# Turning the keys in four pieces and taking their features in pairs, in an attention and expert kernel of one core

## The chip, the cores and the metric

The kernel runs on one core of a Trainium2 chip. The core has five engines that run side by side and wait for each other by semaphores: TensorE (PE in the profile, its weight loads PEld), VectorE (DVE), ScalarE (ACT), GpSimd (POOL) and SyncE (SP), which here only issues DMAs. The metric is the device time of one execution in microseconds; of several executions the median is given.

## The reference, cut to what matters

```python
def phi(x):                                  # q and k: (4, 4, 1088, 32); S1, S2: (8, 32)
    a = np.einsum('rd,bhsd->bhsr', S1, x)
    b = np.einsum('rd,bhsd->bhsr', S2, x)
    return np.einsum('bhsi,bhsj->bhsij', a, b).reshape(*x.shape[:-1], 64)
q_p, k_p = phi(q), phi(k)
kv = np.einsum('bhsf,bhsd->bhfd', k_p, v)
z = np.sum(k_p, axis=2)
num = np.einsum('bhsf,bhfd->bhsd', q_p, kv)
den = np.einsum('bhsf,bhf->bhs', q_p, z)[..., None] + 1e-06
x = (num / den)                              # -> (4352, 128): 4 batches of 1088 tokens, 4 heads of 32
h = x @ w_in                                 # w_in (128, 2048), w_out (2048, 128)
g = np.where(h > 0, h, np.exp(np.minimum(h, 0)) - 1)
out = (g @ w_out).astype(np.float32)
```

q, k and v come as 32-bit floats, S1, S2, w_in and w_out as 64-bit floats. The kernel turns the 64-bit words into 32-bit floats itself, in several elementwise steps.

## The kernel before, in words

Every batch's 1088 tokens are 17 tiles of 64. A group is 8 such tiles (512 columns of x), and the 4352 tokens make nine groups, the last a smaller one. w_in and w_out are cut into eight blocks of 256 of the 2048 hidden units. A step is one group with one block: `mm1` (x times a block of w_in, into the PSUM tiles `h`), ELU on ACT and DVE (`e`, `gg`), and the second product (`o`, or `pa` and `pb`). The order of all work is written out by hand: the program issues instructions to each engine in the order of the source, an engine runs its own in that order, and `at`, `mid` and `late` hang side work on numbered steps.

**The head** comes before the first step. It loads the keys of batch 0 (`hd_k`, two DMAs: tiles 0 to 8 and 9 to 16), turns them on DVE so that features lie on the partitions (`transp`, L281; a tile of the keys is 64 elements of such a transpose in each partition), and multiplies each turned tile with the sketch matrix `Sab` on TensorE (`KF`, L341). Tile `i` of the lower half of the tokens (u = 0, tiles 0 to 8) goes to the columns 0 to 63 of the array, tile `9 + i` of the upper half (u = 1) to the columns 64 to 127. The results of i = 0 to 4 stand in one PSUM bank, those of i = 5 to 8 in another (`abp`), and ACT copies each bank to `abk` (L349). From there the head goes on: the outer products `kp` of the key features on POOL (L324) and DVE (L411), the sums z (`Z_first` L419, `Z` L257, `Z_out` L450), the first query group's features (`q1_first` L516, `q1z_first` L528), its denominators and products (`q2_den`, `q2_out`: `pw` L603, `den` L608 and L609, `an` L611, `qp` L624), `kv` (`KA`, L428), x of the first group (`xg`, L649) and at last the first `mm1` (L686, L257).

**The weights' 64-bit words** are worked on in between. `RA` (L101) is the first step of a block on DVE, `RB` (L106) the second on ACT, and `RC_2`, `RE` the rest. In the kernel before, `q2_den(0, ...)` issues `RA(0)` between `pw` and `den`; `RA(1)` stands between the two halves of `qp`.

**The weight sums.** From group 2 on (and for the last two blocks of group 1) the second product of a step is done as seven half-size products in place of eight (`mm2_seven`, L792). For that POOL makes sums of the weights once, `SS` (`weights7`, L740, four operations for a range of blocks), and sums of `gg` in every step, `tt` (`sums7`, L751 to L756). The first `mm2_seven` of group 2 takes the products in the order p1, p2, p6, p3, p5, p7, p4; p6 reads `tt` of L755, p4 that of L756. POOL's operations stand in one queue, so what `weights7` takes is ahead of the sums of the next step.

The first steps from step 2 on are (1, 0), (1, 1), then blocks 2 to 5 of groups 0 and 1 in turn; steps 12 to 15 are (0, 6), (0, 7), (1, 6), (1, 7), and group 2 begins with step 16. The second product of a step is issued two steps later.

`keep_warm` issues matmuls on constants whose result nobody reads.

Of the kernel before, what the change touches and what calls it, by code (L numbers as in the profile page):

```python
# [22 lines left out]
def _ap(ap: bass.AP, free):  # L23
    return dataclasses.replace(ap, ap=[list(ap.ap[0])] + [list(x) for x in free])
# [3 lines left out]
def kernel(  # L28
# [28 lines left out]
    NP = NC // 2  # L57
    NT = S // 64
    KT = (NT + 1) // 2
# [12 lines left out]
    kT = [const.tile([FD, 2 * KT, 64], F32, name=f"kT{b}") for b in range(2)] * 2  # L72
# [105 lines left out]
    def round_w(f, i, *a):  # L178
        if wide:
            cp, w_in, w_out = order[i]  # L180
            c = slice(0 if w_in else 2 * P, 4 * P if w_out else 2 * P)
            f(raw_w[cp][:, c], W[:, cp, c], *a)

    def RA(i):
        round_w(round_a, i)
# [75 lines left out]
    def keep_warm(n, cols=256, tile=P):  # L261
        ones = nc.const_aps.tensor(1.0, [P, 256], F32)
        for i in range(n):
            for c in range(0, P, tile):
                nc.tensor.matmul(idle[c:c + tile, :cols], ones[:, :tile], ones[:, :cols], skip_group_check=True,  # L265
                                 tile_position=(0, c))
# [13 lines left out]
    def transp(dst, x, b, t0, t1):  # L280
        nc.vector.transpose(dst[b][:, t0:t1, :].rearrange("p t (a c) -> p c t a", c=2), hd[x, b][:, :, t0:t1, :])  # L281
# [4 lines left out]
    def make_SXh():  # L286
        xps = psum.tile([P, 512], F32, name="SXps", tag="aux")
        nc.tensor.matmul(xps[:, :FD], idr[:].rearrange("p x j -> p (x j)"), Sx[:].rearrange("p h d -> p (h d)"))
        nc.scalar.copy(SXh[:], xps[:, :FD])
        nc.gpsimd.tensor_mul(SXh[:].rearrange("p (h d) -> p h d", h=H), SXh[:].rearrange("p (h d) -> p h d", h=H),  # L290
                             _ap(hmask[:], [[1, H], [0, D]]))
# [9 lines left out]
    sps = psum.tile([P, 512], F32, name="sps", tag="aux")  # L301
    nc.tensor.matmul(sps[:, :2 * R], Sx[:].rearrange("p h d -> p (h d)"), ident[:, :2 * R])
    make_SXh()
    transp(kT, "k", 0, 0, 2)
    nc.vector.tensor_mul(Sab[:], _ap(sps[:, :2 * R], [[0, H], [1, 2 * R]]), _ap(bmask[:], [[1, H], [0, 2 * R]]))
    nc.gpsimd.tensor_copy(SW[:, :, :2, :].rearrange("p h x r -> p h (x r)"), Sab[:])

# [26 lines left out]
    def KF(b):  # L334
        ps = [psum.tile([P, 512], F32, name="abp", tag="h", bufs=4) for _ in range(2)]

        part = [(range(5), 0), (range(3), 1)]
        todo = [(i, u) for r, u in part for i in r] + [x for i in range(5, KT) for x in ((i - 2, 1), (i, 0))]
        todo += [(i, 1) for i in range(KT - 2, KT)]
        for i, u in todo:  # L340
            nc.tensor.matmul(ps[i // 5][64 * u:64 * u + 64, 64 * (i % 5):64 * (i % 5) + 64],  # L341
                             kT[b][:, u * KT + i, :], Sab[:].rearrange("p h y -> p (h y)"),
                             skip_group_check=True, tile_position=(0, 64 * u))
        kf_ps.extend(ps)
        ab = feats[b] = work.tile([P, 2, KT, H, R], F32, name="abk", tag="abk", bufs=2)
        for j in range(2):
            t = slice(0, 5) if j == 0 else slice(5, KT)
            n = t.stop - t.start
            nc.scalar.copy(ab[:, :, t].rearrange("p x t h r -> p x (t h) r"),  # L349
                           ps[j][:, :64 * n].rearrange("p (m x r) -> p x m r", x=2, r=R))  # L350
# [172 lines left out]
    def q1z_first():  # L523
        p = psum.tile([P, 512], F32, name="zqp", tag="h", bufs=4)
        for i in range(4):
            for u in range(2):
                b, t = half_tile(0, 2 * i + u)
                nc.tensor.matmul(p[64 * u:64 * u + 64, i * 32:i * 32 + 32].rearrange("p (h r) -> p h r", h=H),  # L528
                                 qT[b][:, t, :], SW[:, :, 2, :], skip_group_check=True, tile_position=(0, 64 * u))
        return p[:, :128].rearrange("p (t h r) -> p h t r", t=4, h=H)  # L530
# [65 lines left out]
    def q2_den(g, zq=None, between=None):  # L596
        m = H * (un[g] if g > 1 else qn[g])
        x = abw[g][:, :m, :]
        pw = pws[g % 2]
        if zq is None:  # L600
            nc.vector.tensor_mul(pw[:, :m, :R], x[:, :, R:2 * R], x[:, :, 2 * R:3 * R])
        else:
            nc.vector.tensor_mul(pw[:, :m, :R].rearrange("p (h t) r -> p h t r", h=H),  # L603
                                 x[:, :, R:2 * R].rearrange("p (h t) r -> p h t r", h=H), zq)
        if between:
            between()
        den = work.tile([P, 8 * H], F32, name="den", tag="den")
        nc.vector.tensor_reduce(den[:, :m], pw[:, :m], axis=AX, op=ADD)  # L608
        nc.vector.reciprocal(den[:, :m], den[:, :m])  # L609
        an = work.tile([P, 8 * H, R], F32, name="an", tag="an")  # L610
        nc.vector.tensor_mul(an[:, :m], x[:, :, R:2 * R], _ap(den[:, :m], [[1, m], [0, R]]))  # L611
        ans[g] = an

    def q2_out(g, parts=1, between=None):
        m = H * qn[g]
        x, an = abw.pop(g), ans.pop(g)
        qp[g] = work.tile([P, 4 * H, R, R], F32, name="qp", tag="qp", bufs=2)
        for i in range(parts):
            if i and between:
                between()  # L620
            h = slice(i * m // parts, (i + 1) * m // parts)
            a_ = an[:, h]
            b_ = x[:, h, :R]
            nc.vector.tensor_mul(qp[g][:, h], _ap(a_, list(a_.ap[1:]) + [[0, R]]),  # L624
                                 _ap(b_, [b_.ap[1], [0, R], b_.ap[2]]))
# [323 lines left out]
            eng.dma_start(rows[b, :, t, :], o[64 * u:64 * u + 64])  # L949


    for t0, t1 in ((2, 5), (KT, KT + 5), (5, KT), (KT + 5, NT)):
        transp(kT, "k", 0, t0, t1)
    KF(0)
    transp(qT, "q", 0, 0, 8)
    zps, zl = Z_first()
# [6 lines left out]
    KO_first(7, KT)  # L963
    keep_warm(1, 96, 64)
    zq = q1z_first()
    q2_den(0, zq, lambda: RA(0))
    q2_out(0, 2, lambda: RA(1))
    KA(0)
    KS_first()
# [53 lines left out]
    def late(n, f, *a):  # L1023
        extra.setdefault((n, 1), []).append((f, *a))
# [75 lines left out]
    late(60, q4, 8)  # L1100

    late(12, weights7, slice(NP - 2, NP))
    late(13, weights7, slice(0, 3))
    late(15, weights7, slice(3, NP - 2))

    N = len(steps)
    for n in range(2, N):
# [95 lines left out]
```

## Time and profile before

| what | us |
|---|---|
| median of 3 executions | 265.42 (265.08 to 265.79) |
| the profiled execution, its own time | 265.08 |
| its span, from the first to the last instruction | 263.3 |
| TensorE busy | 257.8 |
| DVE, ACT, POOL busy | 188.2, 184.5, 168.2 |
| head: start of the first turned keys, start of the first `h` matmul | 4.57, 15.58 |

A line of a timeline has the start in us, the duration in us, the engine, the source line, the operation, the tile written and the tiles read, the shape (partitions x elements) and a count. Where several instructions of one kind follow each other the profile merges them: the start is that of the first, the duration reaches to the end of the last, and x2 is their count. What stands in brackets is the idle time of the engine ahead of it and what ended it. A line of the chain has start, duration, engine, tile and source line. The 32-bit matmuls appear as two passes each, so 18 matmuls are 36 rows.

### The profile page before, as it was taken

How to read it: one execution, taken by the hardware profiler on the slowest of the kernel's cores; microseconds unless marked ns; L12 is line 12 of the kernel's file. 1: busy time of each engine (PE TensorE's matmuls, PEld its weight loads, DVE VectorE, ACT ScalarE, POOL GpSimd, SP SyncE). 2: the span in 40 equal slices, each digit the busy share in tenths (PEclk: the TensorE clock that was granted, in tenths of full speed). 3: DMA queues.
4: the chain of work that ended last, by engine and by line, in shares of the span. 5: the costliest groups of instructions: out<-in, count | busy, mean ns of one | idle time of the engine just before them, and what ended most of it. 6: DMA issues, size and time to landing. Idle time of an engine off the chain costs nothing.

```text
span 263.3 us, 9739 instructions
## 1 busy us (share of the span) xinstructions
PE 257.8 (98%) x4127; PEld 160.5 (61%) x4127; DVE 188.2 (71%) x349; ACT 184.5 (70%) x356; POOL 168.2 (64%) x251
## 2 busy tenths in 40 slices
PE   8899999999999999999999999999999999999994
PEld 7652334354346756667666666665666666667994
DVE  6899999997969997996477676644446445674651
ACT  2479978677567656775587777776777777777793
POOL 4400009105477996798869799888688888998300
PEclk9999999999999999999999999999999999999999
DMA  5997099020011110000100110011001100110011
GB/s 176 339 349 209 2 277 230 1 72 18 2 24 26 26 20 2 2 4 17 31 3 0 29 18 0 2 19 25 3 2 21 23 4 0 18 20 8 2 30 32
DMA packets 26442, 13.73 MB, mean 52 GB/s; under 512 B 19328, under 2 KB 24576, under 8 KB 26400
## 3 DMA queue, kind: packets, MB, share of 16 engines
q1 hardware_dynamic: 25968, 12.76, 18.9%
q8 instruction: 32, 0.52, 0.9%
q10 hardware_dynamic: 368, 0.30, 0.3%
q0 software_dynamic: 64, 0.07, 0.1%
q14 instruction: 10, 0.08, 0.1%
HBM read 10.88 MB, written 2.23 MB: 50 GB/s over the span
## 4 chain that ended last, share of the span: by engine, by line
PE 96%; POOL 1%; DVE 1%; ACT 1%; issue 0%
PE h L257 44%; PE pb L792 16%; PE pa L792 13%; PE o L257 5%; PE pb L768 4%; PE ol L257 3%; PE idle L265 1%; PE kv L428 1%; PE h L686 1%; PE qps L686 1%; POOL kp L324 1%; PE kfps L360 1%; PE qps L576 1%; PE qtp L636 1%; PE kv L257 1%; PE abp L341 1%
## 5 line engine op out<-in xcount | busy, mean ns | idle before, releaser
L257 PE MATMUL h<-xg,W 128*32 128x512 f32 (+3 forms) x904 | 130.7, 539 | 0.4 <-ACT xg L649 0.4
L875 DVE SCALAR_TENSOR_TENSOR gg<-e,h 128x512 f32<-128x512 f32 x128 | 85.6, 683 | 54.1 <-ACT e L869 50.6
L867 ACT ACTIVATE e<-h 128x512 f32<-128x512 f32 x128 | 75.5, 590 | 45.6 <-PE h L257 42.9
L869 ACT ACTIVATE e<-e 128x512 f32<-128x512 f32 x128 | 80.9, 632 | 3.8
L257 PEld LDWEIGHTS h<-xg,W 128*32 128x32 f32 (+1 forms) x904 | 42.6, 122 | 43.2 <-issue 34.9
L754 POOL TENSOR_TENSOR tt<-gg 128x256 f32<-128x256 f32 x50 | 37.0, 741 | 16.4 <-DVE gg L875 16.1
L751 POOL TENSOR_TENSOR tt<-gg 128x256 f32<-128x256 f32 x50 | 36.7, 734 | 5.5 <-DVE gg L875 5.1
L755 POOL TENSOR_TENSOR tt<-tt,gg 128x256 f32<-128x256 f32 x50 | 37.5, 750 | 3.9
L756 POOL TENSOR_TENSOR tt<-gg,tt 128x256 f32<-128x256 f32 x50 | 37.2, 744 | 3.9
L792 PEld LDWEIGHTS pa<-gg,W 128*64 128x64 f32 (+1 forms) x496 | 23.8, 125 | 23.5 <-issue 22.9
L792 PE MATMUL pa<-gg,W 128*64 128x128 f32 (+1 forms) x496 | 30.5, 274 | 0.0
L792 PE MATMUL pb<-tt,SS 128*64 128x128 f32 (+1 forms) x480 | 29.5, 273 | 0.0
L792 PEld LDWEIGHTS pb<-tt,SS 128*64 128x64 f32 (+1 forms) x480 | 22.6, 126 | 0.0
L792 PE MATMUL pa<-tt,SS 128*32 128x128 f32 (+1 forms) x288 | 21.0, 273 | 0.0
L133 POOL TENSOR_TENSOR raw<-raw,tiny 128x512 f32<-128x512 f32 x1 | 1.0, 1044 | 29.4 <-DVE raw L128 29.4
L792 PE MATMUL pb<-tt,W 128*64 128x128 f32 (+1 forms) x256 | 19.8, 273 | 0.0
L792 PE MATMUL pb<-gg,SS 128*64 128x128 f32 (+1 forms) x256 | 19.8, 273 | 0.0
L257 PE MATMUL o<-gg,W 128*32 128x512 f32 x128 | 15.3, 594 | 0.0
L792 PEld LDWEIGHTS pa<-tt,SS 128*32 128x32 f32 (+1 forms) x288 | 13.6, 124 | 0.0
L792 PEld LDWEIGHTS pb<-gg,SS 128*64 128x64 f32 (+1 forms) x256 | 12.7, 125 | 0.0
L792 PEld LDWEIGHTS pb<-tt,W 128*64 128x64 f32 (+1 forms) x256 | 12.6, 125 | 0.0
L768 PE MATMUL pb<-gg,W 128*32 128x256 f32 x192 | 11.5, 380 | 0.0
(163 smaller groups left out, 279.5 us busy)
## 6 DMA issues: line engine op xcount, KB each, us to landing
raw<-in_moe_w_in_dram SPq DMA_DIRECT2D x8, 256.0 KB, 6.6
raw<-in_moe_w_out_dram SPq DMA_DIRECT2D x8, 256.0 KB, 6.4
hd_k<-in_k_dram SPq DMA_DIRECT2D x3, 544.0 KB, 7.3
hd_q<-in_q_dram SPq DMA_DIRECT2D x3, 544.0 KB, 7.9
out_dram<-ob SPq DMA_DIRECT2D x88, 16.0 KB, 1.5
v<-in_v_dram SPq DMA_DIRECT2D x4, 288.0 KB, 6.8
v<-in_v_dram SPq DMA_DIRECT2D x4, 256.0 KB, 8.3
hd_k<-in_k_dram SPq DMA_DIRECT2D x1, 288.0 KB, 3.3
```

The lines of the kernel that those rows point to most:

```text
L257: nc.tensor.matmul(dst[c:c + tile], lhs[:, c:c + tile], rhs, skip_group_check=True, tile_position=(0, c), **kw)
L265: nc.tensor.matmul(idle[c:c + tile, :cols], ones[:, :tile], ones[:, :cols], skip_group_check=True, tile_position=(0, c))
L686: nc.tensor.matmul(ps[w][s * r:s * r + s, 64 * k:64 * (k + m)], lhs, qpT[g, i][rows, o + 2 * k:o + 2 * (k + m), f, :], start=(f == 0 and j ...
L751: nc.gpsimd.tensor_tensor(t[:, 0], b12, b11, op=SUB)
L754: nc.gpsimd.tensor_tensor(t[:, 2], b22, b12, op=SUB)
L755: nc.gpsimd.tensor_tensor(t[:, 1], t[:, 2], b11, op=ADD)
L756: nc.gpsimd.tensor_tensor(t[:, 3], b21, t[:, 1], op=SUB)
L768: nc.tensor.matmul(acc[1][0][r:r + width[0], 256 * hi:256 * hi + 256], lhs[:, w:w + width[0]], gg[:, c, 256 * u:256 * u + 256], start=(cp ...
L792: nc.tensor.matmul(bank[r:r + width[0], P * col:P * col + P], lhs[:, w:w + width[0]], rhs[:, u], start=(first and i in ((0,) if g == 1 els ...
L867: nc.scalar.activation(e, hs[g, cp][c][:, :n], RELU, scale=-1.0)
L869: nc.scalar.activation(e, e, EXP, scale=-1.0)
L875: nc.vector.scalar_tensor_tensor(gs[g, cp][:, c, :n], es[g, cp][:, c, :n], -1.0, hs[g, cp][c][:, :n], op0=ADD, op1=MAX)
```

## The change

The keys of batch 0 are turned in four pieces in place of five: tiles 0 to 2, 9 to 11, 3 to 8, 12 to 16 (before: 0 and 1, 2 to 4, 9 to 13, 5 to 8, 14 to 16). `Sab` is made on DVE after the first piece, in both. `KF` takes the features in pairs, tile i of the lower half and then tile i of the upper half for i = 0 to 8; before, it took the lower tiles 0 to 4 and the upper tiles 0 to 2 first and then mixed the rest. Ahead of the pair i = 3 it issues `keep_warm(1, 96, 64)`, two matmuls of 96 columns, one on each half of the array. `RA(0)` moves from between `pw` and `den` to behind `an`, ahead of the first half of `qp`. `weights7` for blocks 0 to 5 is issued once, in step 15, in place of blocks 0 to 2 in step 13 and blocks 3 to 5 in step 15: POOL has four operations of 384 elements there in place of two times four of 192.

```diff
-    transp(kT, "k", 0, 0, 2)
+    transp(kT, "k", 0, 0, 3)
...
     def KF(b):
         ps = [psum.tile([P, 512], F32, name="abp", tag="h", bufs=4) for _ in range(2)]
-        part = [(range(5), 0), (range(3), 1)]
-        todo = [(i, u) for r, u in part for i in r] + [x for i in range(5, KT) for x in ((i - 2, 1), (i, 0))]
-        todo += [(i, 1) for i in range(KT - 2, KT)]
-        for i, u in todo:
+        for i, u in ((i, u) for i in range(KT) for u in range(2)):
+            if (i, u) == (3, 0):
+                keep_warm(1, 96, 64)
             nc.tensor.matmul(ps[i // 5][64 * u:64 * u + 64, 64 * (i % 5):64 * (i % 5) + 64],
...
-    for t0, t1 in ((2, 5), (KT, KT + 5), (5, KT), (KT + 5, NT)):
+    for t0, t1 in ((KT, KT + 3), (3, KT), (KT + 3, NT)):
         transp(kT, "k", 0, t0, t1)
     KF(0)
...
-    q2_den(0, zq, lambda: RA(0))
+    q2_den(0, zq)
+    RA(0)
     q2_out(0, 2, lambda: RA(1))
...
     late(12, weights7, slice(NP - 2, NP))
-    late(13, weights7, slice(0, 3))
-    late(15, weights7, slice(3, NP - 2))
+    late(15, weights7, slice(0, NP - 2))
```

## The prediction

> **What bounds the kernel now.** I read the page's first two parts, then the chain that ended last, then the timeline of the two places that the diff touches: the head (0 to 15.6 us) and the stretch near 80 us where POOL builds the weight sums.
>
> The page first: busy share by engine, then TensorE's busy tenths in 40 slices.
>
> ```profile
> PE 257.8 (98%) x4127; PEld 160.5 (61%) x4127; DVE 188.2 (71%) x349; ACT 184.5 (70%) x356; POOL 168.2 (64%) x251
> ...
> PE   8899999999999999999999999999999999999994
> ```
>
> TensorE is full from the third slice to the last but one. So a delay moves the end if it comes before TensorE fills up, or if it makes TensorE wait later; other savings on DVE or POOL are worth nothing. The chain in order of time says where it fills up:
>
> ```profile
> 5.04 1.54 PE abp L341 x23
> 6.58 0.02 issue
> 6.61 0.43 ACT abk L349
> ...
> 15.58 2.79 PE h L257 x40
> 18.37 1.02 PE qtp L636 x8
> ```
>
> Until 15.58 us the chain goes from engine to engine; from there on it is almost wholly TensorE's. The key features (abp) stand on it from 5.04. The chain as printed goes on through POOL's kp (7.11 to 9.07), but TensorE takes up its first use of kp at 9.43, right behind other work, so I take the link that hides behind it: last abp matmul, second abk copy, z, zqp, pw, den, an, qp. All of these follow abp.
>
> The timeline of the head, DVE and TensorE:
>
> ```profile
> 4.57 0.31 DVE L281 STREAM_TRANSPOSE kT<-hd_k 128x128 f32<-128x128 f32 x1 [0.57 <-DMA hd_k<-in_k_dram]
> 4.80 0.18 DVE L305 TENSOR_TENSOR Sab<-sps,bmask 128x64 f32<-128x64 f32 x1
> 4.91 0.36 DVE L281 STREAM_TRANSPOSE kT<-hd_k 128x192 f32<-128x192 f32 x1
> 5.21 0.51 DVE L281 STREAM_TRANSPOSE kT<-hd_k 128x320 f32<-128x320 f32 x1
> 5.64 0.67 DVE L281 STREAM_TRANSPOSE kT<-hd_k 128x256 f32<-128x256 f32 x2
> 5.97 0.34 DVE L281 STREAM_TRANSPOSE kT<-hd_k 128x192 f32<-128x192 f32 x1
> 6.23 0.67 DVE L281 STREAM_TRANSPOSE qT<-hd_q 128x512 f32<-128x512 f32 x1
> 5.78 0.33 PE L341 MATMUL abp<-Sab,kT 128*64 128x64 f32 x2
> 6.82 0.22 PE L341 MATMUL abp<-Sab,kT 128*64 128x64 f32 x1
> 7.70 0.69 PE L516 MATMUL abqp<-Sab,qT 128*64 128x64 f32 x16
> ```
>
> Here a tile is 64 elements of a transpose (128x192 is three tiles), and one feature matmul is two passes in these rows (18 matmuls, 36 rows). Two things are to be seen. Passes on one half of the array follow each other 0.058 us apart (the last ones start at 6.65, 6.71, 6.76, 6.82), while the two halves run side by side: abqp, which alternates, puts 16 passes into 0.69 us. And the upper half's stream (u=1) starts at 5.78, 0.06 after its first piece has landed (5.21 + 0.51 = 5.72), and then runs 18 passes almost without a break to 6.82. That stream is what ends abp.
>
> **The change part by part.** No DMA is touched, and SP's, ACT's and POOL's issues stay in their order. DVE loses one transpose, TensorE gains two small warming matmuls, POOL has four operations fewer.
>
> *Pieces and pairs.* The new pieces have 3, 3, 6 and 5 tiles: 192, 192, 384 and 320 elements; the last holds tiles 12 to 16, which the upper half needs from its fourth tile on. Start-to-start times on DVE: 0.26 to 0.30 for 192 (5.97 to 6.23, 4.91 to 5.21), 0.33 for 256, 0.43 for 320, 0.11 for Sab. For 384 there is no row; from 256 and 320 I estimate 0.48 (0.45 to 0.53). So: first piece 4.57, Sab 4.85, second piece 4.96 (landed 5.32), third 5.24, fourth 5.72, landed 5.72 + 0.51 = 6.23 (6.16 to 6.32). TensorE starts 0.06 after a landing: the upper half's tiles 0 to 2 at about 5.38, its tile 3 at about 6.28. The first pass behind a wait takes 0.107 to the next (5.78 to 5.88 before), then 0.058 each: six tiles are twelve passes, and the last starts at 6.28 + 0.107 + 10 x 0.058 = 6.97. Before it was 6.82. So abp ends 0.15 us later (0.08 to 0.24): the upper half starts 0.4 earlier than before, but stops after three tiles, and the larger last piece is behind it with twelve passes instead of eight. The pairing as such gives nothing, since the two halves already ran side by side; it costs the lower half its lead, which nobody needs. Nothing lies beside this on the path: both abk copies, kp, z and all that follows move by the same amount.
>
> *Warming matmuls.* Two matmuls, four passes of 96 columns, beside each other in pairs: the same ones at 8.31 take 0.37. They stand between the third and fourth pair, at about 5.8 to 6.0, while TensorE waits for the fourth piece until 6.28. Cost nothing; if that cover of 0.3 were gone, 0.2.
>
> *First rounding step.* Rows of the first query group:
>
> ```profile
> 9.62 0.29 DVE L603 TENSOR_TENSOR pw<-abq,zqp 128x128 f32<-128x128 f32 x1 [0.23 <-PE zqp L528]
> 9.82 0.33 DVE L101 TENSOR_SCALAR W<-raw 128x256 uint32<-128x256 uint32 x1
> 10.07 0.29 DVE L608 TENSOR_REDUCE den<-pw 128x16 f32<-128x144 f32 x1
> 10.39 0.25 DVE L609 RECIPROCAL den<-den 128x16 f32<-128x16 f32 x1
> ```
>
> The step fills the gap in which den waits for pw. A dependent operation starts about 0.03 after its producer's end (10.36 to 10.39), up to 0.10 where two waits meet, so without the step den comes at 9.94 to 10.01: 0.06 to 0.13 gained. Behind an, the step fills the same kind of gap ahead of qp: it starts 0.20 after an and holds DVE 0.20 to 0.25 (the second such step runs 11.62 to qp at 11.82), so qp comes 0.40 to 0.45 after an's start and not 0.33: 0.07 to 0.12 lost. I take zero (0.06 either way). Queued behind the moved step is only qp; who waits for its result is ACT's second step at 11.55, which it still leads by 0.3.
>
> *Weight sums.* POOL, with the one TensorE row that counts:
>
> ```profile
> 77.79 0.59 POOL L740 TENSOR_TENSOR SS<-W 128x192 f32<-128x192 f32 x1
> 79.57 0.60 POOL L740 TENSOR_TENSOR SS<-W,SS 128x192 f32<-128x192 f32 x1
> 80.12 0.75 POOL L751 TENSOR_TENSOR tt<-gg 128x256 f32<-128x256 f32 x1
> 81.65 0.74 POOL L755 TENSOR_TENSOR tt<-tt,gg 128x256 f32<-128x256 f32 x1
> 82.47 0.74 POOL L756 TENSOR_TENSOR tt<-gg,tt 128x256 f32<-128x256 f32 x1
> 83.89 0.40 PE L792 MATMUL pa<-tt,SS 128*32 128x128 f32 x8
> ```
>
> The four sums of blocks 0 to 2 leave 64.59 to 67.02, where POOL then idles 2.4 us for gg at 69.45, so nothing is gained there. They join the four at 77.79, each now 384 elements. 128, 192 and 256 elements take 0.46, 0.60 and 0.73, so 384 takes about 1.00 (0.92 if the slope falls as for longer operations). Four of them need about 3.97 in place of 2.33: everything behind on POOL comes 1.64 us later (1.3 to 1.7). The sums of the first block of group 2 are queued there: the one that TensorE's third product reads (L755) ended at 82.39 and now ends at 84.03. TensorE wants it at 83.89. Add 0.06 for the signal and 0.05 for the first pass behind a wait: TensorE stands 0.22 us (0 to 0.35). The last product needs L756 at 84.84 and comes at 84.98, so no second wait. POOL had 1.35 us of idle time before 85.25 and takes the lag up there. Behind it TensorE is full, so the 0.22 stays.
>
> Sum: 0.15 + 0 + 0 + 0.22 = 0.37 us. The profiled execution took 265.08, the lowest of the three shown, so it would become 265.45; the median is 265.42, so I say 265.8.
>
> **Rules weighed.** TensorE's clock: the 256-column warming passes at the start follow each other 0.43 us apart (3.05 to 3.47), later 512-column ones take as long, so the array starts at half rate and is at full rate for abp. The Trainium skill, "TensorE: Matmul & The Clock Gate" (Part 1), says that the rate is released after a busy window of about 3.4 us that runs freely, and falls only after idle time of that order. By the rule the new gaps of 0.3 us cannot lower the rate, but an execution whose window lies later must be busy through just this stretch; the sum would be the same by rule and row unless that happens. No run shows it here.
>
> **The rivals.**
> - *Slower, by the clock.* TensorE would now stand from about 5.15 to 5.38 and 6.0 to 6.28. If that delays the release of the rate beyond abqp, twelve passes cost 0.05 more each and abqp's eight on a half as well: about 1.0 us, with the 0.37 some 1.4, so 266.8. It decides if the first passes at 6.28 are over 0.1 apart. Against it: the head before stands 0.36 at 8.48 without losing the rate.
> - *Slower, by POOL.* At 92.20 one POOL sum took 1.59 in place of 0.73, beside a DVE product of two SBUF tensors (qp at 91.56). If one of the longer sums meets such a one, 0.9 more goes straight to TensorE's wait: 266.7. It decides from 0.45 on top. Against it: DVE's rows from 78 to 82 are transposes, gg and kp, and at 79 to 80 POOL showed 0.60 beside them.
> - *Not slower.* The transposes come at the low ends (abp + 0.08), POOL's long sums take 0.92 (wait 0), the moved step gains 0.06: 265.4. For it: the terms are small and DVE drops an operation.
> - *The change does nothing in the head*, because the printed chain through POOL's kp is the true one: kp waits for the first abk copy, which moves as much. Then the same 265.8.
>
> **How the numbers follow.** 0.3% is 0.8 us, about what a measurement of this kernel can tell from no change. My forecast (265.5 to 266.15), the do-nothing rival in it: 0.56. Not slower (265.0 to 265.5): 0.13, of it 0.03 below 264.6. Slower by clock, POOL or an unseen wait of the same size: 0.31, nearly all over 266.2. So faster 0.03, same 0.66, slower 0.31. The range runs from 265.1 to 266.8: it leaves out about 0.06 below and 0.12 above.
>
> **What would show it.** The last transpose of keys lands near 6.23 and abp's last pass starts near 6.97; ACT's second abk copy at 7.23 (before 7.08); TensorE's first h at about 15.73; four POOL sums of about 1.00 from 77.9 on; a wait of TensorE for POOL of about 0.2 in the first block of group 2, near 84. Wrong if the upper half's stream ends before 6.82, if no wait for POOL appears, or if passes after 6.28 are 0.107 apart.

## The result, and the profile after

| | us |
|---|---|
| before, median of 22 executions | 265.38 (265.08 to 265.79) |
| after, median of 22 executions | 265.94 (265.64 to 266.73) |
| after / before | 1.0023, 95% interval 1.0016 to 1.0029 |
| profiled execution before, span | 265.08, 263.3 |
| profiled execution after, span | 265.99, 264.2 |

The kernel is slower by 0.56 us in the medians, under the 0.8 that the prediction set as the bound of a change, and inside its range of 265.1 to 266.8. The forecast was 265.8. The size agrees; the working behind it does not in every term, so that part of the agreement is luck, and that is what the rest is about.

The two profiled executions differ by 0.91, more than the medians do. The one of before happens to be the fastest of its 22. So the terms below are read from the place where they arise, not from the two spans.

The page of after, as above for before: busy share by engine and TensorE's busy tenths.

```profile
span 264.2 us, 9742 instructions
...
PE 258.9 (98%) x4131; PEld 160.5 (61%) x4131; DVE 188.2 (71%) x348; ACT 184.5 (70%) x356; POOL 167.5 (63%) x247
...
PE   8899999999999999999999999999999999999994
```

Nothing is to be seen at this scale: TensorE is as full as before, and the four rows more are the two warming matmuls. The chain of after has its first long TensorE piece of `h` at 16.16, where before it was at 15.58:

```profile
6.97 0.44 ACT abk L350
...
16.16 2.77 PE h L257 x40
```

The head has therefore lost 0.56 to 0.58. The timeline of DVE and ACT in the head shows the first part of it:

```profile
4.56 0.38 DVE L281 STREAM_TRANSPOSE kT<-hd_k 128x192 f32<-128x192 f32 x1 [0.56 <-DMA hd_k<-in_k_dram]
4.86 0.18 DVE L305 TENSOR_TENSOR Sab<-sps,bmask 128x64 f32<-128x64 f32 x1
5.21 1.23 DVE L281 STREAM_TRANSPOSE kT<-hd_k 128x192 f32<-128x192 f32 x3 [0.16 <-DMA hd_k<-in_k_dram]
6.36 0.68 DVE L281 STREAM_TRANSPOSE qT<-hd_q 128x512 f32<-128x512 f32 x1
6.97 0.84 ACT L350 COPY abk<-abp 128x320 f32<-128x320 f32 x2 [1.33 <-PE abp L342]
```

The second piece starts at 5.21, not at 4.96. DVE stands 0.16 for a DMA, the one that brings the upper half of the keys. The three pieces then run on to 6.44 without a break (the last of them starts at 5.97), and the second copy to `abk` comes at 7.44 (before 7.08). The second part of the loss stands at the end of the head, in the weight loads of the first group's x (`xps`). Before:

```profile
14.06 0.18 PEld L643 LDWEIGHTS xps<-qpT,kvS 64*32 64x32 f32 x16
14.65 0.16 PEld L265 LDWEIGHTS idle<-const-float32-1.0 128*32 128x32 f32 x8 [0.41 <-issue]
```

After:

```profile
14.45 0.17 PEld L644 LDWEIGHTS xps<-qpT,kvS 64*32 64x32 f32 x12
15.06 0.14 PEld L644 LDWEIGHTS xps<-qpT,kvS 64*32 64x32 f32 x4 [0.45 <-issue]
15.62 0.16 PEld L265 LDWEIGHTS idle<-const-float32-1.0 128*32 128x32 f32 x8 [0.41 <-issue]
```

Sixteen rows in one run have become twelve and four, with 0.45 of idle time between them that no engine released ("issue"). `xps` begins 0.39 late and the `idle` loads behind it 0.97 late; most of that lies in the time in which TensorE waits for the copies of `xg` on ACT anyway, and the first `h` is 0.56 late.

The third part is on POOL and TensorE near 84 us. POOL, TensorE and its weight loads in the timeline of after:

```profile
78.35 1.01 POOL L741 TENSOR_TENSOR SS<-W 128x384 f32<-128x384 f32 x1
81.38 1.02 POOL L741 TENSOR_TENSOR SS<-W,SS 128x384 f32<-128x384 f32 x1
82.36 0.73 POOL L752 TENSOR_TENSOR tt<-gg 128x256 f32<-128x256 f32 x1
83.86 0.74 POOL L756 TENSOR_TENSOR tt<-tt,gg 128x256 f32<-128x256 f32 x1
83.99 0.62 PE L793 MATMUL pa<-gg,W 128*32 128x128 f32 x16
84.65 0.43 PE L793 MATMUL pa<-tt,SS 128*32 128x128 f32 x8
84.65 0.16 PEld L793 LDWEIGHTS pa<-tt,SS 128*32 128x32 f32 x8 [0.31 <-POOL tt L756]
```

The sum that the third product reads ends at 84.60, and the product starts 0.05 behind it. Before, the product followed 0.44 after the first of the two ahead of it (83.45 to 83.89); here that would be 83.99 + 0.44 = 84.43, so the wait costs 0.22.

### The profile page after: what moved, and what is told of

Same layout as the page of the kernel before. It is cut to its first block, busy times and chain, and to the rows that moved or that the text cites. A ratio compares the mean times of both kernels' runs of the same rounds, so it can differ in the third digit from the quotient of the medians.

```text
span 264.2 us, 9742 instructions
## 1 busy us (share of the span) xinstructions
PE 258.9 (98%) x4131; PEld 160.5 (61%) x4131; DVE 188.2 (71%) x348; ACT 184.5 (70%) x356; POOL 167.5 (63%) x247
## 3 DMA queue, kind: packets, MB, share of 16 engines
HBM read 10.88 MB, written 2.23 MB: 50 GB/s over the span
## 4 chain that ended last, share of the span: by engine, by line
PE 95%; DVE 2%; POOL 1%; issue 0%; ACT 0%
PE h L257 44%; PE pb L793 16%; PE pa L793 13%; PE o L257 5%; PE pb L769 4%; PE ol L257 3%; PE idle L265 1%; PE kv L429 1%; PE h L687 1%; PE qps L687 1%; POOL kp L324 1%; PE kfps L361 1%; PE qps L577 1%; PE kv L257 1%; PE abp L342 1%; PE qtp L637 0%
```

## The experiments

Each kernel is an edit of before, and the line numbers differ by one or two between them. The ratio is that of the kernel to before, with its 95% interval. A ratio of 1.001 is 0.27 us. The first four shared one chip (before 265.39), the next four another (before 265.44), the last four a third (before 265.43).

| kernel | median us | ratio |
|---|---|---|
| e1, weight sums alone | 265.67 | 1.0007 (0.9998 to 1.0016) |
| e2, rounding step alone | 265.48 | 1.0002 (0.9993 to 1.0011) |
| e3, keys alone | 265.86 | 1.0016 (1.0008 to 1.0025) |
| e4, before again | 265.39 | 1.0001 (0.9993 to 1.0010) |
| e5, keys without warming | 265.61 | 1.0013 (1.0000 to 1.0025) |
| e6, lower pieces first | 265.45 | 1.0011 (0.9999 to 1.0023) |
| e7, before with two more warming matmuls | 265.69 | 1.0010 (1.0002 to 1.0019) |
| e8, all weight sums in step 13 | 265.82 | 1.0017 (1.0008 to 1.0025) |
| e9, five pieces, small one last | 265.47 | 0.9999 (0.9990 to 1.0008) |
| e10, e11, e12: e5, e7, e6 once more, one execution each | 265.66, 265.57, 265.41 | |

### One part at a time

The weight sums alone:

```diff
-    late(13, weights7, slice(0, 3))
-    late(15, weights7, slice(3, NP - 2))
+    late(15, weights7, slice(0, NP - 2))
```

> The kernel before with one part of the change: the weight sums of blocks 0 to 5 in one go in step 15. Theory A (the loss is a new wait of TensorE for GpSimd in group 2's first block, plus a later last piece of keys): about +0.22 us, ratio 1.0008, and TensorE waits 0.2 for the sum of L755 near 84, with four sums of about 1.0 us ahead of it. Theory B (the whole loss lies in the head, by a later release of TensorE's clock): no change, ratio 1.0000, whatever the wait looks like.

The view of waits in e1 has the wait that after has, and before has not:

```profile
PEld pa L792 <- POOL tt L755: 0.3, 1, 0.3
```

(The columns behind the colon are idle us in all, how often, the longest.) ACT's first `e` behind it is 0.50 later than in before (86.59 against 86.09), the one ahead of it 0.27 (84.28 against 84.01), so 0.23 is added here. By its median e1 loses 0.28, by its ratio 0.19; the interval of the ratio still takes in 1, so it is the rows that show this part.

The rounding step alone:

```diff
-    q2_den(0, zq, lambda: RA(0))
+    q2_den(0, zq)
+    RA(0)
```

> The kernel before with the first rounding step behind an, ahead of qp, and nothing else. Theory A and B alike: no change within 0.06 us; the first half of qp starts 0.40 to 0.45 after an starts, and den 0.33 to 0.40 after pw starts. If this part carried the loss, it would be +0.3 or more.

The timeline of DVE in e2:

```profile
9.65 0.29 DVE L603 TENSOR_TENSOR pw<-abq,zqp 128x128 f32<-128x128 f32 x1 [0.23 <-PE zqp L528]
10.04 0.30 DVE L608 TENSOR_REDUCE den<-pw 128x16 f32<-128x144 f32 x1
...
10.66 0.29 DVE L611 TENSOR_TENSOR an<-abq,den 128x128 f32<-128x128 f32 x1
10.87 0.29 DVE L101 TENSOR_SCALAR W<-raw 128x256 uint32<-128x256 uint32 x1
11.08 0.69 DVE L624 TENSOR_TENSOR qp<-an,abq 128x512 f32<-128x512 f32 x1
```

`den` comes 0.39 after `pw` (before 0.45) and `qp` 0.42 after `an` (before 10.68 to 11.01, 0.33): 0.06 gained and 0.09 lost. From `pw` to `qp` it is 1.43 in place of 1.39, and near 84 us ACT's `e` is only 0.01 later than before (84.02 against 84.01). The interval lies around 1. In these runs the step is worth nothing that can be told from zero.

The keys alone (pieces, pairs and the warming matmuls):

```diff
-    transp(kT, "k", 0, 0, 2)
+    transp(kT, "k", 0, 0, 3)
...
-        for i, u in todo:
+        for i, u in ((i, u) for i in range(KT) for u in range(2)):
+            if (i, u) == (3, 0):
+                keep_warm(1, 96, 64)
...
-    for t0, t1 in ((2, 5), (KT, KT + 5), (5, KT), (KT + 5, NT)):
+    for t0, t1 in ((KT, KT + 3), (3, KT), (KT + 3, NT)):
```

> The kernel before with the four pieces, the pairs and the two warming matmuls, and nothing else. Theory A: +0.15 (0.08 to 0.24) where TensorE's rate is released as early as in the profile of before; the last piece of keys lands near 6.23 to 6.45, and the upper half's tile 3 starts 0.06 behind it. Theory B: +0.35 or more, and its first passes are 0.10 apart well beyond 5.8 in the profile, as in the profile of the changed kernel, while the other kernels of this job show passes 0.058 apart from 5.1 on.

And before once more, as a measure of what two profiles of one kernel differ by:

> The kernel before, unchanged, for its profile: ratio 1.0000. Theory A: the time at which TensorE's rate is released differs from execution to execution of one kernel, so this profile and the two of e1 and e2, which have the same head up to pw, show different release times, some of them after 5.0. Theory B: all three show it before 5.0.

The three ratios give 0.0007 + 0.0002 + 0.0016 = 0.0025 above 1, the whole change 0.0023: within their intervals the parts add up, and the keys are the largest. DVE in e3:

```profile
5.23 1.23 DVE L281 STREAM_TRANSPOSE kT<-hd_k 128x192 f32<-128x192 f32 x3
```

The late second piece is there without the other two parts, and the last pass of `abp` is at 7.20 as against 7.18 in after. The row shows no idle time ahead of the piece because `Sab` itself came later here, at 4.95; in e6 below, with the same `Sab`, the second piece starts at 5.09. Neither expectation held: 0.0016 is 0.42 us, more than theory A's 0.24, and the passes are 0.058 apart early, against theory B. e4 gave 1.0001 and in its profile a surprise: 265.89 for the program that took 265.08 above. That answers a question about the clock. In the head's timeline one matmul of 128 columns (`SXps`) shows at which rate TensorE runs just ahead of the key features; in the order before, after, e3, e4:

```profile
4.76 0.28 PE L288 MATMUL SXps<-Sx,idr 128*128 128x128 f32 x1
```
```profile
4.92 0.42 PE L288 MATMUL SXps<-Sx,idr 128*128 128x128 f32 x1
```
```profile
4.97 0.28 PE L288 MATMUL SXps<-Sx,idr 128*128 128x128 f32 x1
```
```profile
5.11 0.42 PE L288 MATMUL SXps<-Sx,idr 128*128 128x128 f32 x1
```

At 0.28 the passes of `abp` follow each other at 0.058 from the start. At 0.42 they are 0.107 apart until about 6.2 in after and about 6.4 in e4, and 0.058 from there on. Unchanged code (before, e4) shows both, so what decides is the execution and not the edit. In the kernel before a late release is dear: the second `abk` copy starts at 7.72 in e7, 7.59 in e4 and 7.38 in e1, against 7.08. A part of that, 0.15 in e4 and e7, is there at `Sab` already (4.96 in place of 4.80); counted from `Sab` the late release costs 0.3 to 0.5. With the new pieces it costs nothing in the one late case seen: 7.44 with the late release (after), 7.46 with the early one (e3). There the pieces set the end: in after, e3, e5 and e10 the second copy starts 2.23 to 2.24 behind the second piece, whenever the rate was released.

The times say the same. Each execution on record has a mean granted clock, the share of its full rate that TensorE was given. It is 0.997 or 0.998 in 16 of the 85 executions of before that ran beside the experiments; their median is 265.88, that of the other 69 is 265.37. Of the 22 executions of the changed kernel six have it, with 265.96 against 265.92. I take the low mean as a sign of a late release, since in e7 and e9, both 0.997, the passes are 0.107 apart until about 6.7 and 6.4. It is a rough sign: e4 was late with 1.000, and e8 has 0.998 with passes 0.058 apart from the start.

### What in the keys costs the time

e5 takes the warming matmuls out of e3:

```diff
         for i, u in ((i, u) for i in range(KT) for u in range(2)):
-            if (i, u) == (3, 0):
-                keep_warm(1, 96, 64)
```

> Four pieces and pairs as in e3, without the two warming matmuls. The prediction's theory (they are hidden and cost nothing): as e3, ratio 1.0016, and the products xps still broken after 12 of 16 rows. Rival (two more matmuls in TensorE's stream move a pause of 0.3 to 0.4 us, for which the profile names no releaser, from behind xps into it): xps whole again as in the kernels before, xg and the first h 0.1 to 0.2 earlier than in e3 against abk, ratio 1.0010 to 1.0013.

e6 in addition turns the rest of the lower half ahead of the upper half's first piece:

```diff
-    for t0, t1 in ((KT, KT + 3), (3, KT), (KT + 3, NT)):
+    for t0, t1 in ((3, KT), (KT, KT + 3), (KT + 3, NT)):
```

> As e5, with the second and third piece exchanged: tiles 3 to 8 are turned while the DMA of the upper half is still under way. Theory A' (the head loses because DVE stands for the upper half's keys, which land near 5.2, before the second piece): no idle time of DVE ahead of a key piece, the last piece lands near 6.25 and not 6.45, abp's last pass starts at 6.98 (0.2 earlier than in e3, counted from Sab), and the time is 0.15 to 0.25 us below e5's. If the pairs or the size of the last piece were the whole cause: as e5.

The timeline of e5, DVE and ACT:

```profile
5.24 1.23 DVE L281 STREAM_TRANSPOSE kT<-hd_k 128x192 f32<-128x192 f32 x3 [0.15 <-DMA hd_k<-in_k_dram]
...
7.00 0.84 ACT L348 COPY abk<-abp 128x320 f32<-128x320 f32 x2 [1.81 <-PE abp L340]
```

and of e6:

```profile
5.09 1.22 DVE L281 STREAM_TRANSPOSE kT<-hd_k 128x384 f32<-128x384 f32 x3
...
6.85 0.84 ACT L348 COPY abk<-abp 128x320 f32<-128x320 f32 x2 [1.26 <-PE abp L340]
```

With the lower pieces first DVE has no idle time ahead of them, the run of three starts 0.15 sooner, and the copies to `abk` come 0.15 sooner. The data of the lower tiles are there (the first DMA brought them); those of the upper half are not. Two single executions more give the same with a larger step: in e10, which is e5, DVE waits again, the second piece starts at 5.31 and the second `abk` copy at 7.55; in e12, which is e6:

```profile
5.00 1.21 DVE L281 STREAM_TRANSPOSE kT<-hd_k 128x384 f32<-128x384 f32 x3
...
6.75 0.84 ACT L348 COPY abk<-abp 128x320 f32<-128x320 f32 x2 [1.36 <-PE abp L340]
```

> e5's kernel once more, for its profile. If the longer pause ahead of the idle matmuls behind xps (0.92 in e5) belongs to the kernel: again 0.8 to 1.0. If it comes and goes: 0.4 as in the kernels before. DVE stands again for the upper half's keys: second piece near 5.2 whatever Sab does.

> e6's kernel once more, for its profile. If the absence of the pause belongs to the kernel: again 0.4 ahead of the idle matmuls and xps whole; if it comes and goes, a pause of 0.3 to 0.5 more at the same place. No idle time of DVE ahead of the upper half's pieces in either case.

In time, e6's median is that of before (265.45 and 265.44), e5's 0.16 above e6's, and e12 took 265.41 beside e10's 265.66. The ratios of e5 and e6 cannot be told apart, since two of e6's twelve executions took 266.76 and 266.86 and two of e5's 266.58 and 266.97. So the wait for the DMA is shown as the cause of the late pieces, and the 0.15 to 0.33 on the path by the rows; for the gain in time of the other order there are medians and single executions only.

Nor does e5's time decide about the warming matmuls that it leaves out. By the medians e3 loses 0.47 to its own before and e5 0.17, but the ratios are 1.0016 and 1.0013, with intervals that overlap almost wholly.

### The warming matmuls

e7 adds two warming matmuls to before and changes nothing else. They stand where TensorE waits anyway, behind ones that are there already:

```diff
     KO_first(7, KT)
-    keep_warm(1, 96, 64)
+    keep_warm(2, 96, 64)
     zq = q1z_first()
```

> The kernel before with two more warming matmuls at 8.4 us, where TensorE waits 0.36 for DVE anyway. If extra matmuls are free there: ratio 1.0000 and xps whole. If a pause stands at a fixed place of TensorE's instruction stream: xps broken after 12 of 16 rows with 0.3 to 0.4 without a releaser ahead of the last four, and 0.05 to 0.15 us more in the end (ratio 1.0002 to 1.0006).

> e7's kernel once more, for its profile. If the break of xps after 12 rows belongs to the two more matmuls: again 12 and 4 rows with 0.3 to 0.45 between them. If it comes and goes: xps whole. TensorE's rate may be released early or late; if late by chance only, this profile may show abp's passes 0.058 apart from the start.

The weight loads of `xps` in e11, and then in e10 (no additional matmuls):

```profile
14.23 0.17 PEld L643 LDWEIGHTS xps<-qpT,kvS 64*32 64x32 f32 x12
14.69 0.14 PEld L643 LDWEIGHTS xps<-qpT,kvS 64*32 64x32 f32 x4 [0.30 <-issue]
```

```profile
14.53 0.18 PEld L642 LDWEIGHTS xps<-qpT,kvS 64*32 64x32 f32 x16
15.12 0.16 PEld L265 LDWEIGHTS idle<-const-float32-1.0 128*32 128x32 f32 x8 [0.41 <-issue]
```

All four profiles with two more matmuls on TensorE ahead of `xps` (after, e3, e7, and e11, which is e7) show it broken after twelve rows, with 0.30 to 0.45 of idle time that no engine released; none of the ten without does. That the matmuls stand elsewhere in e7 than in e3 makes no difference to the place of the break. From the start of `xps` to the first ELU of the first group the lag behind before grows by 0.03 in e11, by 0.08 in e7, by 0.09 in e3, by 0.19 in after; without the two matmuls this stretch agrees within 0.02 in all ten. A fixed position in the instruction stream would explain it: two matmuls are four weight loads more, and the break stands four rows ahead of the end of `xps`. That is argued and not shown; the cause stays open. In e5 another pause, ahead of the `idle` matmuls, was 0.92 long where it is 0.41 to 0.52 otherwise; in e10, the same program, it was 0.41, so the kernel does not set that one, and e5's first ELU was not later for it.

e7's ratio of 1.0010 is not the price of the matmuls alone: three of its eleven executions have the low mean clock of a late release, of the before beside it four of 35. By its median e7 loses 0.25, more than the rows give, and what the two matmuls cost in time stays open between 0.03 and about 0.3.

### The weight sums at another time

If the sums are in the way in step 15, they could all stand in step 13, where POOL idles:

```diff
-    late(13, weights7, slice(0, 3))
-    late(15, weights7, slice(3, NP - 2))
+    late(13, weights7, slice(0, NP - 2))
```

> The kernel before with the weight sums of blocks 0 to 5 in one go, in step 13 and not 15. If what costs in e1 is the place (ahead of the first sums of group 2) and not the length of the operations: no wait of TensorE for GpSimd near 84, ratio 1.0000, since GpSimd stands idle for 2.4 us there before and the longer sums take 4.0 in place of 2.4 of the 4.9 us. If long sums cost by themselves: as e1, 1.0007.

Neither expectation held: 1.0017. No wait for POOL is left near 84, but a new one has come earlier. Timeline of before, DVE:

```profile
66.08 0.48 DVE L601 TENSOR_TENSOR pw<-abw 128x128 f32<-128x128 f32 x1
...
67.55 1.22 DVE L666 TENSOR_TENSOR qp<-an,abw 128x1024 f32<-128x1024 f32 x1
```

and of e8, with POOL and TensorE:

```profile
66.08 0.75 DVE L601 TENSOR_TENSOR pw<-abw 128x128 f32<-128x128 f32 x1
67.88 1.92 DVE L666 TENSOR_TENSOR qp<-an,abw 128x1024 f32<-128x1024 f32 x1
67.65 1.06 POOL L740 TENSOR_TENSOR SS<-W,SS 128x384 f32<-128x384 f32 x1
71.69 0.67 PE L686 MATMUL qps<-qpT,kvq 64*64 64x64 f32 x12 [0.38 <-DVE qpT L673]
```

`pw` and `qp` are products of two SBUF tensors on DVE. Beside POOL's longer sums they take 0.75 and 1.92 in place of 0.48 and 1.22. 0.97 more on DVE is enough that TensorE stands 0.38 for `qpT`. This agrees with the Trainium skill, "GPSIMD Engine Reference" (1. Specifications), which says that GpSimd shares its SBUF interfaces with VectorE and that the two contend where a DVE instruction reads two SBUF inputs. It is the price of the rival "slower, by POOL", found in another place than it was looked for.

Even the 0.48 of before is not undisturbed: `pw` runs beside two of the shorter sums there. In after, where step 13 has no sums of blocks 0 to 5, it takes

```profile
66.62 0.27 DVE L602 TENSOR_TENSOR pw<-abw 128x128 f32<-128x128 f32 x1
```

So the change does free 0.2 us of DVE near 66 us, but nobody waits for it: the lag of ACT's `e` behind before is 0.54 on either side of it.

### A version that beats both?

e9 keeps the split weight sums and the rounding step of before, has five pieces with the small one last, no additional matmuls, and the lower tiles 0 to 4 first:

```diff
-    transp(kT, "k", 0, 0, 2)
+    transp(kT, "k", 0, 0, 3)
...
-        part = [(range(5), 0), (range(3), 1)]
-        todo = [(i, u) for r, u in part for i in r] + [x for i in range(5, KT) for x in ((i - 2, 1), (i, 0))]
-        todo += [(i, 1) for i in range(KT - 2, KT)]
+        todo = [(i, 0) for i in range(5)] + [(0, 1), (5, 0)] + [(i, 1) for i in range(1, 6)]
+        todo += [x for i in range(6, KT) for x in ((i, 1), (i, 0))]
...
-    for t0, t1 in ((2, 5), (KT, KT + 5), (5, KT), (KT + 5, NT)):
+    for t0, t1 in ((3, 6), (KT, KT + 4), (KT + 4, NT), (6, KT)):
```

> The kernel before with other pieces and another order, to see whether a version beats both: tiles 0 to 2, Sab, 3 to 5, 9 to 12, 13 to 16, 6 to 8; lower tiles 0 to 4 first, then the halves in turn; no warming matmuls. By the terms that the runs confirmed (0.30 for 192 elements, 0.33 for 256, nothing of the upper half touched before 5.2, 0.058 a pass) the upper half's stream starts at 5.72 and ends at 6.76 (before 6.82): 0.06 less than before, ratio 0.9998, too little to be told from no change by these rounds; if the wait for the upper half's keys is not what costs, it is slower, like e5 (1.0013).

0.9999 (0.9990 to 1.0008): no gain that could be told from zero. Its profile has a late release, so the expected 6.76 cannot be read in it (the last pass is at 7.25). No kernel of this study is faster than before. Not tried was an earlier load of the upper half of the keys, which is what the wait points to.

## Why the prediction was right or wrong

**Pieces and pairs: the direction right, the size not.** The step that failed is "first piece 4.57, Sab 4.85, second piece 4.96 (landed 5.32)". It chained DVE's starts as if nothing but DVE were in the way. But the second piece is now the first of the upper half, and that half has a DMA of its own. The issue stands in the timeline of ACT's queue in before:

```profile
1.38 0.66 ACTq L78 DMA_DIRECT2D hd_k<-in_k_dram  x1
```

and the landing in its list of DMA issues (us from issue to landing at the end of the line):

```profile
hd_k<-in_k_dram ACTq DMA_DIRECT2D x1, 256.0 KB, 3.8
```

1.38 + 3.8 is 5.18, and the piece started at 5.21 to 5.24; in e10 the DMA landed at 5.29 and the piece started at 5.31. In the kernel before nobody waits for that DMA, because the piece of tiles 2 to 4 runs until just then: its first upper piece also starts at 5.21. The change takes away the work that hid the landing. All that follows is late by the same amount: last piece 5.97 and not 5.72, landed 6.44 and not 6.23, last pass 7.18 and not 6.97, second copy 7.44 and not 7.23. The cost on the path is 7.44 − 7.08 = 0.36 (0.38 in e3), not 0.15, and outside the bounds of 0.08 to 0.24 as well. The copies bear out that it is this start that counts: in after, e3, e5 and e10 they keep the same distance from it. The rest of the term held. From the second piece's start to the last one's it was to be 0.76 (4.96 to 5.72, with 0.48 estimated for six tiles) and was 0.76 (5.21 to 5.97), and from the landing to the second copy it was to be 1.00 (6.23 to 7.23) and was 1.00 (6.44 to 7.44).

**Warming matmuls: not free.** That 0.3 of waiting covers them where they stand holds: from the last piece to the last pass it is 1.21 with them (after, e3) and without (e5). What was not seen is that two instructions more shift something 8 us later; the 0.2 "if that cover of 0.3 were gone" was given for another reason and covers the 0.03 to 0.19 of the rows by luck.

**First rounding step: right.** `qp` comes 0.04 later behind `pw` in e2, of which 0.01 is left near 84; predicted was zero with 0.06 either way.

**Weight sums: right.** Four sums of 1.01 to 1.02 (predicted about 1.00); the wait named at its place; the third product's sum at 84.60, which is 0.57 after the predicted 84.03, of it 0.54 the delay that comes from the head; the cost 0.22 as predicted, and 0.19 to 0.28 in e1's times. The exact hit is partly luck: the prediction's own figures, 84.03 + 0.06 + 0.05 − 83.89, make 0.25. Measured, the sum ends 0.17 behind the time at which TensorE wants it, and 0.05 pass from there to the product's start.

**The sum.** Predicted 0.15 + 0 + 0 + 0.22 = 0.37. Measured by the rows: 0.36 + 0.19 + 0.01 + 0.22 = 0.78, and ACT's first `e` behind the wait is 0.79 late (86.88 against 86.09). At the end of TensorE's work the lag is 0.77; the rest of the 0.91 between the two profiles comes behind TensorE's last matmul, where e4, the same program as before, loses 0.15 as well. By the medians the change costs 0.56, by the ratio 0.0023 x 265.4 = 0.61. The rows give more than the times, and I put that down to two things. The profile of before had the early release of the rate (`abk` 7.08), while the times of before contain executions with a late one (7.38 to 7.72), for which the new head loses next to nothing; by the low mean clock these are about a fifth, 16 of 85. And after's own profile has the dearest of the four broken `xps`. That the forecast of 265.8 came within 0.14 of 265.94 is therefore no proof of its sum: two terms were short by 0.21 and by up to 0.19.

**The rivals.** "Slower, by the clock" falls: the test it named did not come true. Behind the last piece of keys only the first passes are 0.107 apart, as the forecast had it too, and then they are 0.058 apart, although the release was late; and unchanged code shows the late release too. "Slower, by POOL" falls for after, where POOL's sums were undisturbed, and its price is real in e8. "Not slower" falls with the interval, which lies above 1. Whether the chain's link through POOL's `kp` is the true one stays open, since both links follow `abk`.

## What to carry to other kernels

When pieces of a load are reordered, write the landing of each DMA (issue plus time to landing) beside the start that you compute for its reader: an engine's order can be hiding a landing that no wait in the old profile shows. Where side work is put into an idle gap of one engine, look for what other engines do beside it; the gap in step 13 was free on POOL and dear on DVE. And profile the unchanged kernel twice before a difference of a few tenths between two traces is given a cause.

## What the runs showed of the hardware

- The rate of TensorE's start varies from execution to execution of the same program: in two profiles of before the passes of `abp` were 0.058 apart from the first on, or 0.107 apart until about 6.4 us. The Trainium skill, "TensorE: Matmul & The Clock Gate" (Part 1), describes a window of about 3.4 us that runs freely, so that the release lies differently from run to run; the rows agree. The prediction wrote that no run showed it; these do. Counted from `Sab`, the price at `abk` is 0.3 to 0.5 us where TensorE's passes set the end of the head (e1, e4, e7), and nothing measurable where the transposes do (after).
- Two matmuls more on TensorE broke a run of sixteen weight loads after the twelfth in four of four profiles, with 0.30 to 0.45 of idle time without a releaser, and in none of ten without them. Why is not known.
- POOL's sums of 384 elements slowed two DVE products of two SBUF tensors: `qp` from 1.22 alone to 1.92, and `pw` from 0.27 alone (0.48 beside sums of 192 elements) to 0.75. A `qp` of the same size that reads one of its inputs from PSUM (`qa`, at 115.08 in before) took 1.19 with POOL at work beside it.
